# RetNet attention and a leaky-ReLU feed-forward block: second-layer trunk products kept in PSUM over a chunk, and a fourth product by two levels

## The chip, the cores and the metric

The kernel runs on one core of one Trainium2 chip, in fp32. The metric is the device time of one execution in microseconds; a kernel's time is the median of several runs.

## The reference

A recurrent RetNet block feeds two dense layers. What matters here is the second half:

```
state = gamma * state + k_t v_t^T          # per batch and head, 768 positions
y_t   = scale * q_t state
x = y as (3072 tokens, 512)                # 4 batches, 768 positions, 8 heads of 64
h = x @ w_in                               # 512 -> 2048
g = max(0.01 h, h)
out = g @ w_out                            # 2048 -> 512
```

## The kernel before, in words

**Chunks and units.** The 768 positions are cut into six chunks `c` of 128, each with 4 x 128 = 512 tokens; the hidden width 2048 is cut into four units `u` of 512. For each chunk and unit the first layer gives a 512 x 512 hidden block, and the second layer adds its product with the unit's rows of `w_out` to the chunk's output `o` (four blocks of 128 x 512).

**One level and two levels.** Each 512 x 512 product is done with seven products of half-size blocks instead of eight (Winograd's form of Strassen's method). A product done *at one level* is four fp32 matmuls of 128x128 by 256 columns. A product done *by two levels* is cut into seven again: seven fp32 matmuls of 128x128 by 128 columns. A profile shows each fp32 matmul as two MATMUL records and two LDWEIGHTS records.

**The main loop.** Chunks 0 and 1 are done in a first part. From about 249 us on, the loop over `n` (0 to 15; `c, u = 2 + n // 4, n % 4`) does the rest. Step `n` issues, in each engine's program order:

1. `differences(g)`: four VectorE subtractions on the hidden block of unit `n`.
2. `inner(n+1, 0)`: the first layer of the *next* unit, group 0, four products by two levels (28 fp32 matmuls) in PSUM banks 0 to 3; ScalarE copies and VectorE adds take them out. `outer(n+1, 0)` combines them on VectorE.
3. With `u < 2` and another chunk to come ("visiting"), `joint_visit`: the attention output of a pair of batches for the next chunk.
4. `sums_of_x` or `differences` for the next chunk's first-layer operands, on VectorE.
5. The second layer of unit `n`. In steps 0 to 3 and 15 this is `output`: seven products at one level. In steps 4 to 14 (`by_leaves`) four products (M1, M5, M6, M7: the *trunk*) are at one level, and three (M2, M3, M4: the *leaves*) by two levels. `leaf_sums` makes the leaves' operands on GpSimd, four subtractions of 128x384.
6. `scores_of_pair`: attention scores and state sums of the next pair, where there is one.
7. `inner(n+1, 1)`: the first layer, group 1, three products by two levels (21 matmuls), again in banks 0 to 3; then `outer(n+1, 1)`, five VectorE adds and four ScalarE activations.
8. The last trunk product and the leaves (`leaf_steps`), then their addition to `o`.

The order is written out by hand: each engine works through its own queue in the order in which the program issues. In `inner_steps` and `leaf_steps` the order of products is `INNER`: M1, M5, M4, M6, M2, M3, M7; four banks are used, and after M1 ScalarE copies M1's sum from the first bank into the fourth, where M6 and M7 add to it:

```
INNER = (("M1", 0, 0, 0), ("M5", 1, 3, 2), ("M4", 2, 2, 4), ("M6", 3, 4, 3), ("M2", 0, 1, 1),
         ("M3", 1, 5, 5), ("M7", 3, 6, 6))
```

(name, bank among the four, block of the weights, block of the moving operand). VectorE takes M3 once and M7 twice; ScalarE takes the others.

**Trunk and leaves before.** `trunk` puts M1, M5 and M6 + M7 into three banks A, C, B (5, 7, 4), copies A into B after M1, and every unit is added to `o` by VectorE (`o[:, 1]`, `o[:, 2:4]`, and in `trunk_taken` `o[:, 0]` and `o[:, 1:4:2]`). The leaves use banks 6, 7, 2 and 5. Their results lie in SBUF; a DMA issued by GpSimd adds them to `o` (L1283, `accum_op`), except at the chunk's last unit, where VectorE adds them and the output is stored.

**Leaf weights.** Each leaf product needs seven weight blocks per row, three of the original and four sums. In steps 0 to 3 `sums_of_rows` makes the sums on VectorE, four instructions of 128x384 for a unit, and `keep` writes them to DRAM (`leaf_kept`); `load_rows` loads three rows of 448 KB in each step with leaves. The first-layer weights of each step are loaded on the same SP queue (`wa`, `wb` from `kept`).

Of the kernel before, what the change touches and what calls it, by code (L numbers as in the profile page):

```python
# [22 lines left out]
def kernel(  # L23
# [334 lines left out]
    def scores_of_pair(c, b, banks=None, mid=None):  # L358
# [28 lines left out]
        for j in range(2):  # L387
            am = work.tile([128, 2, HP // 2, 2, C // 2], FP32, tag=f"am{j}", name=f"am{j}_{c}_{b}")
            nc.vector.tensor_tensor(
                out=am.rearrange("p b m i t -> p (b m i) t"),  # L390
                in0=at[j].rearrange("p b m i t -> p (b m i) t"),
                in1=mask[:, 0].unsqueeze(1).to_broadcast([128, 2 * HP, C // 2]), op=ALU.mult)
            weights.append(am)
# [7 lines left out]
        if not last:  # L401
            state_of[p] = halves_of_states.pop(0)
            plus(state_of[p], mid, sums[1])
        mid_of[p] = old, mid
# [9 lines left out]
    def joint_visit(c, b, banks=None):  # L414

        later = following(c, b) if c > JOINED else None
        banks = banks or [[bank[k] for k in at] for at in ((1, 2), (0, 7))]
# [193 lines left out]
    def plus(out, a, b):  # L611
        nc.vector.tensor_tensor(out=out, in0=a, in1=b, op=ALU.add)  # L612

    def minus(out, a, b):
        nc.vector.tensor_tensor(out=out, in0=a, in1=b, op=ALU.subtract)  # L615
# [13 lines left out]
    def differences(x, t, last=True):  # L629

        minus(t[:, 0], x[:, 1], x[:, 0])
        minus(t[:, 1], x[:, 3], t[:, 0])
        minus(t[:, 2], x[:, 2], t[:, 1])
        if last:
            last_difference(x)

    def last_difference(x):
        minus(x[:, 1], x[:, 3], x[:, 1])
# [169 lines left out]
    last_three = {}  # L808
# [9 lines left out]
    def new_g(c, u):  # L818
        i = slot[0]
        slot[0] = 1 - i  # L820
        both = work.tile([128, 7, 2, N], FP32, tag=f"g{i}", name=f"g_{c}_{u}")
        last_three[c, u] = both[:, 2:5]
        return u, both[:, 0:4], Reversed(both)
# [309 lines left out]
    def sums_of_x(c, group):  # L1133
# [3 lines left out]
        for blocks, made in (((x[:, 0:1], made[:, :, 0:1]), (t, made[:, :, 1:4])) if group == 0 else  # L1137
# [5 lines left out]
            minus(b12, b22, b12)  # L1143
# [40 lines left out]
    leaf_kept = [dram.tile([128, 3, 7, C], FP32, name=f"leaf_kept_{u}") for u in range(NU)]  # L1184
# [3 lines left out]

    def leaf_rooms():

        free = [flat_of(unit(k)[:, 2:5]) for k in (1, 3, 5)]
        spare = [x2_place[0][:, 21 * C :], streamed_flat[0][:, 21 * C :]]
        more = [spare[i // 2][:, ds(i % 2 * 3 * C, 3 * C)] for i in range(4)]
        return free, spare, [x.rearrange("p (q n) -> p q n", q=3) for x in more]

    def rows_of(u):

        if u < NU - 1:
            return [((0, 3, 1), unit(2 * u + 1)[:, 2:5])]
        return [((0, 3, 2), units[2 * u + 1][1]), ((1, 2, 1), last_s4)]  # L1200

    def sums_of_rows(u):

        free, _, more = leaf_rooms()
        if u == NU - 1:
            more = more[0:2] + [x[:, 7 * C : 10 * C].rearrange("p (q n) -> p q n", q=3)
                                for x in free[0:2]]
        bases = []
        for at, blocks in rows_of(u):
            which = slice(*at)  # L1210
            a11, a21, a12, a22 = (blocks[:, :, k, ts(m, C)] for k in range(2) for m in range(2))
            r = [x[:, which] for x in more]
            plus(r[0], a21, a22)
            minus(r[1], r[0], a11)
            minus(r[2], a12, r[1])
            minus(r[3], a11, a21)
            bases.append((which, blocks))

        def keep():
            for which, blocks in bases:  # L1220
# [4 lines left out]
            for j, r in enumerate(more):  # L1225
                nc.sync.dma_start(out=leaf_kept[u][:, :, 3 + j], in_=r)
        return keep

    def load_rows(n):

        free, spare, _ = leaf_rooms()
        leaf_weights[:] = [x[:, 0 : 7 * C].rearrange("p (j n) -> p j n", j=7)
                           for x in (free[0], free[1], spare[1])]
        for to, kept_rows in zip(leaf_weights, (leaf_kept[at_of(n)[1]][:, i] for i in range(3))):
            nc.sync.dma_start(out=to, in_=kept_rows)

    leaf_weights = []

    def by_leaves(n):
        return n >= NU and n < N2 - 1  # L1240

    def leaf_sums(n):

        free, spare, _ = leaf_rooms()
        made = [x.rearrange("p (q n) -> p q n", q=3)
                for x in (free[0][:, 7 * C : 10 * C], free[1][:, 7 * C : 10 * C],
                          spare[0][:, 0 : 3 * C])]
        three = last_three[at_of(n)]
        b11, b12, b21, b22 = (three[:, :, k, ts(h, C)] for k in range(2) for h in range(2))
        for out, a, b in ((made[0], b12, b11), (made[1], b22, made[0]), (made[2], b21, made[1]),  # L1250
                          (b12, b22, b12)):
            nc.gpsimd.tensor_tensor(out=out, in0=a, in1=b, op=ALU.subtract)
        return [b11, b21, *made, b22, b12]

    def leaf_steps(n, moving):

        ps = [bank[i][:, 0 : 3 * C].rearrange("p (i n) -> p i n", i=3) for i in (6, 7, 2, 5)]
        results = leaf_results()
        for m, q, j, s in INNER:
            for i in range(3):  # L1260
                nc.tensor.matmul(ps[q][:, i], lhsT=leaf_weights[i][:, j], rhs=moving[s][:, i],  # L1261
# [6 lines left out]
            elif m == "M7":  # L1268
                plus(results[:, :, 3], results[:, :, 3], ps[3])
                plus(results[:, :, 2], results[:, :, 2], ps[3])  # L1270
# [5 lines left out]
    def leaf_results():  # L1276
        return flat_of(unit(5)[:, 2:5]).rearrange("p (i q n) -> p i q n", i=3, q=4)

    def leaf_results_taken(c, o, final):

        results = leaf_results()
        if not final:
            nc.gpsimd.dma_start(out=o[:, 0:3].rearrange("p i k n -> p (i k n)"),  # L1283
                                in_=results.rearrange("p i q n -> p (i q n)"), accum_op=ALU.add)
            return
        for i in range(3):
            plus(o[:, i], o[:, i], results[:, i].rearrange("p (k h) n -> p k (h n)", k=2))
            nc.sync.dma_start(out=out[c, i], in_=o[:, i])

    def trunk(c, o, part, first, final):  # L1290

        u, g, gd = part
        ps = {x: room[x] for x in "ABC"}
        for m, x, sa, rhs, start in (("M1", "A", 0, g[:, 0], True), ("M5", "C", 4, gd[:, 0], True),
                                     ("M6", "B", 5, gd[:, 1], False),
                                     ("M7", "B", 1, g[:, 1], False)):
            for i in range(2):
                for k in range(2):
                    nc.tensor.matmul(ps[x][:, i, :], lhsT=block(2 * u + 1, sa)[:, k, ts(i, 128)],  # L1299
                                     rhs=rhs[:, k, :], start=(start and i == 0 and k == 0),  # L1300
                                     stop=(k == 1), skip_group_check=True)
            if m == "M1":
                nc.scalar.copy(out=ps["B"], in_=ps["A"])  # L1303
            elif m == "M6":
                if first:
                    nc.scalar.copy(out=o[:, 1], in_=ps["B"])
                else:
                    plus(o[:, 1], o[:, 1], ps["B"])
            elif m == "M7":
                yield  # L1310
                if first:
# [299 lines left out]
```

## Time and profile before

| | |
|---|---|
| median of 3 runs | 633.93 us (633.60 to 633.94) |
| profiled execution | 633.81 us, span 632.1 us |
| TensorE busy | 624.7 us, 99% |
| VectorE busy | 498.1 us, 79% |
| ScalarE busy | 283.5 us, 45% |
| GpSimd busy | 81.4 us, 13% |
| granted TensorE clock | 1.00 |
| a step with neither visit nor scores | 22.54 us (n = 6, 7, 10, 11, 13, 14) |
| steps 4, 5, 8, 9 | 27.0, 27.0, 27.0, 25.7 us |

PE is TensorE's matmuls and PEld its weight loads, DVE is VectorE, ACT ScalarE, POOL GpSimd, SP the queue that issues most DMAs. `Lnnn` is a line of the kernel, and where a helper such as `plus` (L612) or `minus` (L615) records the instruction, all its users share that line. In a chain, each row is a start, a duration and what ran. In a timeline, each row is a start, a duration, engine, line, operation, output and inputs, shape, count, and in brackets how long the engine had been idle and for whom it waited. A step's length is TensorE's time from one start of inner group 0 to the next.

### The profile page before, as it was taken

How to read it: one execution, taken by the hardware profiler on the slowest of the kernel's cores; microseconds unless marked ns; L12 is line 12 of the kernel's file. 1: busy time of each engine (PE TensorE's matmuls, PEld its weight loads, DVE VectorE, ACT ScalarE, POOL GpSimd, SP SyncE). 2: the span in 40 equal slices, each digit the busy share in tenths (PEclk: the TensorE clock that was granted, in tenths of full speed). 3: DMA queues.
4: the chain of work that ended last, by engine and by line, in shares of the span. 5: the costliest groups of instructions: out<-in, count | busy, mean ns of one | idle time of the engine just before them, and what ended most of it. 6: DMA issues, size and time to landing. Idle time of an engine off the chain costs nothing.

```text
span 632.1 us, 15063 instructions
## 1 busy us (share of the span) xinstructions
PE 624.7 (99%) x6284; PEld 570.5 (90%) x6284; DVE 498.1 (79%) x803; ACT 283.5 (45%) x559; POOL 81.4 (13%) x98
## 2 busy tenths in 40 slices
PE   8999999999999999999999999999999999999997
PEld 5888888888888889899999999999998999999996
DVE  5679769889979976668887768799848889866765
ACT  5876646347443114352442452634434424544540
POOL 2000000000011010101000033313033023033200
PEclk9999999999999999999999999999999999999999
DMA  8941325547772998295964888998479579689724
GB/s 330 404 138 34 133 67 208 163 145 226 260 276 81 334 350 289 89 347 168 340 209 157 280 293 250 342 293 260 157 240 306 159 230 278 206 263 271 192 45 116
DMA packets 103219, 141.18 MB, mean 223 GB/s; under 512 B 4328, under 2 KB 82024, under 8 KB 103152
## 3 DMA queue, kind: packets, MB, share of 16 engines
q1 hardware_dynamic: 101552, 132.53, 63.3%
q0 software_dynamic: 1296, 7.08, 5.6%
q8 instruction: 49, 0.80, 0.5%
q10 hardware_dynamic: 304, 0.62, 0.3%
q14 instruction: 18, 0.15, 0.1%
HBM read 108.49 MB, written 24.64 MB: 211 GB/s over the span
## 4 chain that ended last, share of the span: by engine, by line
PE 90%; DMA 5%; ACT 2%; DVE 2%; issue 0%; SPq 0%; DVEq 0%; ACTq 0%
PE bank L1348 26%; PE bank L1299 12%; PE bank L668 11%; PE bank L1261 8%; PE C_h L668 4%; PE B_o L668 4%; PE A_h L668 4%; PE A_o L668 4%; PE C_o L668 4%; PE B_h L668 4%; PE D_o L668 2%; PE D_h L668 2%; DMA x_words<-in_weights_dram 1%; DMA wa<-kept 1%; DMA in<-in_kv_dram 1%; PE bank L371 1%
## 5 line engine op out<-in xcount | busy, mean ns | idle before, releaser
L612 DVE TENSOR_TENSOR made<-made,bank 128x512 f32<-128x512 f32 (+1 forms) x96 | 56.1, 617 | 39.9 <-PE bank L1348 35.9
L1348 PEld LDWEIGHTS bank<-x,wb 128*128 128x128 f32 x672 | 77.6, 192 | 1.1 <-ACT bank L1352 0.3
L1348 PE MATMUL bank<-x,wb 128*128 128x128 f32 x672 | 77.9, 275 | 0.1
L612 DVE TENSOR_TENSOR o<-o,bank 128x512 f32<-128x512 f32 (+3 forms) x75 | 55.2, 767 | 24.3 <-ACT bank L782 6.2
L615 DVE TENSOR_TENSOR g<-g 128x512 f32<-128x512 f32 x96 | 64.1, 688 | 5.3 <-ACT g L1390 0.6
L1348 PE MATMUL bank<-x,wa 128*128 128x128 f32 x512 | 67.6, 275 | 0.0
L1299 PE MATMUL bank<-g,w 128*128 128x256 f32 x288 | 66.1, 382 | 0.7 <-DVE x L468 0.7
L1348 PEld LDWEIGHTS bank<-x,wa 128*128 128x128 f32 x512 | 62.8, 192 | 0.3
L1299 PEld LDWEIGHTS bank<-g,w 128*128 128x128 f32 x288 | 53.2, 190 | 8.0 <-DVE x L468 1.1
L1348 PE MATMUL bank<-t,wa 128*128 128x128 f32 x384 | 53.4, 275 | 0.1
L1348 PEld LDWEIGHTS bank<-t,wa 128*128 128x128 f32 x384 | 48.0, 192 | 0.3 <-DMA wa<-kept 0.3
L612 DVE TENSOR_TENSOR g<-made 128x512 f32<-128x512 f32 x64 | 44.0, 709 | 3.0
L1352 ACT COPY bank<-bank 128x512 f32<-128x512 f32 (+1 forms) x32 | 16.6, 520 | 60.1 <-PE bank L1348 59.8
L1390 ACT ACTIVATE g<-g 128x512 f32<-128x512 f32 x64 | 38.5, 631 | 8.2 <-DVE g L612 8.2
L668 PE MATMUL bank<-g,w 128*128 128x256 f32 x168 | 38.0, 382 | 0.0
L668 PEld LDWEIGHTS bank<-g,w 128*128 128x128 f32 x168 | 31.3, 190 | 4.2
L668 PE MATMUL bank<-g,last 128*128 128x256 f32 (+1 forms) x148 | 32.6, 375 | 0.0
L668 PEld LDWEIGHTS bank<-g,last 128*128 128x128 f32 x148 | 27.0, 190 | 3.9 <-DVE g L615 0.4
L1261 PE MATMUL bank<-g,w 128*128 128x128 f32 x176 | 26.8, 275 | 0.0
L668 PE MATMUL A_h<-x,w 128*128 128x256 f32 x112 | 26.6, 380 | 0.0
L1303 ACT COPY bank<-bank 128x512 f32<-128x512 f32 x11 | 6.3, 570 | 41.1 <-PE bank L1299 41.1
L1283 POOL DMA_DIRECT2D o<-w x9 | 8.1, 903 | 125.2 <-DVE g L615 65.6
(255 smaller groups left out, 1234.8 us busy)
## 6 DMA issues: line engine op xcount, KB each, us to landing
wa<-kept SPq DMA_DIRECT2D x16, 1344.0 KB, 9.4
raw<-in_weights_dram SPq DMA_DIRECT2D x31, 512.0 KB, 4.4
wb<-kept SPq DMA_DIRECT2D x16, 896.0 KB, 5.5
w<-leaf_kept SPq DMA_DIRECT2D x22, 448.0 KB, 4.6
wa<-kept SPq DMA_DIRECT2D x16, 448.0 KB, 6.1
wb<-kept SPq DMA_DIRECT2D x16, 448.0 KB, 6.3
o<-w POOLq DMA_DIRECT2D x9, 768.0 KB, 9.2
out_dram<-o SPq DMA_DIRECT2D x23, 256.0 KB, 2.5
```

The source lines that it names most:

```text
L371: nc.tensor.matmul(at[j][ts(h, 64), n, m, i], lhsT=x[ts(j, 64), 1, a, ts(h, 64)], rhs=x[ts(j, 64), 0, a, ts(h, 64)], start=(n == 0 and a = ...
L612: nc.vector.tensor_tensor(out=out, in0=a, in1=b, op=ALU.add)
L615: nc.vector.tensor_tensor(out=out, in0=a, in1=b, op=ALU.subtract)
L668: nc.tensor.matmul(to, lhsT=block(w, sa)[:, k, ts(i, 128)], rhs=rhs[:, k, a:z], start=(first and (i == 0 or split) and n == 0 and k == 0), ...
L1261: nc.tensor.matmul(ps[q][:, i], lhsT=leaf_weights[i][:, j], rhs=moving[s][:, i], start=(i == 0 and m in ("M1", "M5", "M4")), stop=True, sk ...
L1283: nc.gpsimd.dma_start(out=o[:, 0:3].rearrange("p i k n -> p (i k n)"), in_=results.rearrange("p i q n -> p (i q n)"), accum_op=ALU.add)
L1299: nc.tensor.matmul(ps[x][:, i, :], lhsT=block(2 * u + 1, sa)[:, k, ts(i, 128)], rhs=rhs[:, k, :], start=(start and i == 0 and k == 0), sto ...
L1303: nc.scalar.copy(out=ps["B"], in_=ps["A"])
L1348: nc.tensor.matmul(ps[q][:, i], lhsT=w[:, j, i], rhs=part_of(moving[i], s), start=(i == 0 and m in ("M1", "M5", "M4")), stop=True, skip_gr ...
L1352: nc.scalar.copy(out=ps[3], in_=ps[0])
L1390: nc.scalar.activation(g[:, i], g[:, i], AF.Prelu, alpha=0.01)
```

## The change

From step 2 to step 14, M1, M5 and M6 stay at one level, but their sums stay in banks A, C and B over all units of a chunk that are done this way: only the first unit's matmul starts the sum. `trunk_taken` takes them out once, at the chunk's last such unit: one ScalarE copy and five VectorE additions. M7 becomes a fourth leaf. The leaves have four blocks in every place where they had three, use banks 6, 2, 0 and 3, and start at step 2 instead of step 4. For units 2 and 3 of chunk 2 (`ON_CHIP`) the weight sums are used from SBUF; GpSimd makes them, in steps 1 and 3. The results of a chunk's first unit are written straight to `o`; those of later units are added to `o` by one VectorE addition of 128x2048 (`add_results`) in the following step. The chunk's stores move to the first step of the next chunk (`finish_chunk`). `outer(n+1, 0)` comes after `joint_visit` or `sums_of_x`; `sums_of_x(c+1, 1)` comes after inner group 0; with `u` = 2 or 3 GpSimd's `leaf_sums` waits for the last of VectorE's `sums_of_x`. The second half of the masks comes last in `scores_of_pair`. The core of the diff (`plus`, `minus`, `differences` and `sums_of_x` also return their last instruction now):

```diff
+    ON_CHIP = range(2, NU)
+    def by_leaves(n):
+        return ON_CHIP[0] <= n < N2 - 1
-        return n >= NU and n < N2 - 1
 def rows_of(u):
-            return [((0, 3, 1), unit(2 * u + 1)[:, 2:5])]
+            return [(slice(0, 4), unit(2 * u + 1)[:, 1:5])]
+        first, second = units[2 * u + 1][0:2]
+        return [(slice(0, 1), first[:, 1:2]), (slice(1, 4, 2), second), (slice(2, 3), last_s4)]
+    def sums_of_rows(u, engine=nc.vector):
+        if u in ON_CHIP:
+            flat = free[1].rearrange("p (r q n) -> p r q n", r=4, q=4)
+            parts = [(slice(0, 4), slice(0, 4), flat)]
+        else:
+            rows = [(slice(0, 1), blocks[:, 0:1]), (slice(1, 4), blocks[:, 1:4])]
...
+        for n in range(4):
+            for which, blocks in rows:
...
+                engine.tensor_tensor(out=r[n], in0=a, in1=b, op=ALU.subtract if n else ALU.add)
 def load_rows(n):
+        for i in range(4):
+            to = free[(1, 3)[i // 2]][:, ds(i % 2 * 7 * C, 7 * C)]
...
+            nc.sync.dma_start(out=to, in_=leaf_kept[at_of(n)[1]][:, i])
+    def leaf_sums(n, behind=None):
+        made = [of_four(leaf_rooms()[x]) for x in ("x2", "wb", "u2")]
+        four = last_four[at_of(n)]
...
+            op = nc.gpsimd.tensor_tensor(out=out, in0=a, in1=b, op=ALU.subtract)
+            if behind is not None:
[...]
+                behind = None
+    TARGETS = (3, 0, 1, 2)
 def leaf_steps(n, moving):
-        ps = [bank[i][:, 0 : 3 * C].rearrange("p (i n) -> p i n", i=3) for i in (6, 7, 2, 5)]
+        ps = [bank[i].rearrange("p (i n) -> p i n", i=4) for i in (6, 2, 0, 3)]
...
+        plus(results[:, :, 2], results[:, :, 2], ps[3])
+        plus(results[:, 2], results[:, 2], results[:, 3])
+        if at_of(n)[1] > 0:
+            unadded.append(lambda: plus(flat_of(os[at_of(n)[0]]), flat_of(os[at_of(n)[0]]),
+                                        results.rearrange("p i q n -> p (i q n)")))
+    def finish_chunk(c):
+        add_results()
+        for i in range(4):
+            nc.sync.dma_start(out=out[c, i], in_=os[c][:, i])
+    def trunk(n, part):
+        first = n == ON_CHIP[0] or u == 0
+        for x, sa, rhs in (("A", 0, g[:, 0]), ("C", 4, gd[:, 0]), ("B", 5, gd[:, 1])):
...
+                                     rhs=rhs[:, k, :], start=(first and i == 0 and k == 0),
+    def trunk_taken(n, o):
+        a, ab, abc = (flat_of_k(leaf_results(n)[:, i]) for i in range(3))
+        nc.scalar.copy(out=a, in_=room["A"])
+        plus(o[:, 0], o[:, 0], room["A"])
+        plus(ab, a, room["B"])
+        plus(abc, ab, room["C"])
+        plus(o[:, 2], o[:, 2], ab)
+        plus(o[:, 1:4:2], o[:, 1:4:2], abc.unsqueeze(1).to_broadcast([128, 2, 2, N]))
 # the loop over n
+        last_leaves = leaves and (u == NU - 1 or n + 2 == N2)
+        if u > 0:
+            add_results()
         if more:
             differences(*gs[n][1:])
...
+        elif leaves and u == NU - 1:
+            behind = sums_of_x(c + 1, 1)
+        if more:
             outer(n + 1, 0)
+        if leaves and u == 0:
+            finish_chunk(c - 1)
+            os[c] = new_o(c)
+        if visiting and u == 1:
+            behind = differences(*xs[c + 1])
+        elif c + 1 < NC and u == 2:
+            behind = sums_of_x(c + 1, 0)
+        if leaves:
+            moving = leaf_sums(n, behind if not scores_next else None)
+            trunk(n, part)
...
+        if last_leaves:
+            trunk_taken(n, os[c])
+        if scores_next and leaves:
+            scores_of_pair(*scores_next, [bank[i] for i in (1, 6, 2, 3)], second_mask_last=True)
...
+        if n in (0, 1):
+            keep.append(sums_of_rows(n))
+        if n in (1, 3):
+            keep.append(sums_of_rows({1: 2, 3: 3}[n], nc.gpsimd))
         if more:
             inner(n + 1, 1)
...
+        if leaves:
+            leaf = leaf_steps(n, moving)
+            last_one = n + 2 == N2
+            for count, ready in ((1, 1), (1, 1), (2, 2)) if last_one else ((4, 3), (1, 1)):
+                products(leaf, count)
+                for _ in range(ready):
+                    later.pop(0)()
+            if last_one:
+                differences(*gs[n + 1][1:])
+            products(leaf, 8)
+            if last_one:
+                add_results()
```

## The prediction

> **What bounds the kernel now.** First the busy shares, then the chain that ended last, then one stretch in order of time on each engine. The shares:
>
> ```profile
> PE 624.7 (99%) x6284; PEld 570.5 (90%) x6284; DVE 498.1 (79%) x803; ACT 283.5 (45%) x559; POOL 81.4 (13%) x98
> ```
>
> TensorE hardly idles, so an edit gains only if it takes work from TensorE. The chain, over step n = 7 of the main loop (start us, us, what):
>
> ```profile
> 427.79 6.25 PE bank L1348 x56
> 434.04 5.18 PE bank L1299 x24
> 439.22 4.69 PE bank L1348 x42
> 443.91 1.73 PE bank L1299 x8
> 445.64 4.69 PE bank L1261 x42
> 450.33 6.25 PE bank L1348 x56
> ```
>
> Weight loads are counted with matmuls: x56 is 28 of each. A step is inner group 0 (6.25), three trunk products (5.18), inner group 1 (4.69), the fourth trunk product M7 (1.73), three leaf products (4.69): 22.54 us, without a gap. From these lines a one-level product costs 5.18/3 = 1.73 us, a two-level one 7 x 0.2233 = 1.56 us. VectorE, GpSimd and one uncontended reference in the same stretch (start, duration, idle before):
>
> ```profile
> 236.26 0.55 DVE L615 TENSOR_TENSOR x<-x 128x384 f32<-128x384 f32 x1
> ...
> 428.76 2.88 DVE L615 TENSOR_TENSOR g<-g 128x512 f32<-128x512 f32 x4
> 431.56 1.36 DVE L615 TENSOR_TENSOR x<-x 128x384 f32<-128x384 f32 x1
> 432.95 2.50 DVE L615 TENSOR_TENSOR x<-x,x 128x384 f32<-128x384 f32 x2
> 435.38 1.35 DVE L615 TENSOR_TENSOR x<-x 128x384 f32<-128x384 f32 x1
> ...
> 443.35 1.62 DVE L612 TENSOR_TENSOR made<-made,bank 128x384 f32<-128x384 f32 x3 [0.91 <-PE bank L1348]
> ```
>
> ```profile
> 431.19 1.31 POOL L1252 TENSOR_TENSOR w<-g 128x384 f32<-128x384 f32 x1 [0.87 <-DVE g L615]
> 432.58 1.19 POOL L1252 TENSOR_TENSOR w<-g,w 128x384 f32<-128x384 f32 x1
> ...
> 465.54 1.00 POOL L1252 TENSOR_TENSOR w<-g,w 128x384 f32<-128x384 f32 x1
> ```
>
> Two things are to be seen. In a step with u = 3, VectorE reaches the eviction of inner group 1 with 0.91 us to spare, and that is all its slack. And `sums_of_x` beside GpSimd's `leaf_sums` takes 1.36 us an instruction instead of 0.55, GpSimd 1.2 to 1.3 instead of 1.00.
>
> [...] the two `mask` products out of PSUM at 465.14 beside GpSimd take 1.29 together. [...] the trace has 688 ns at 512 and 1214 at 1024[...].
>
> **The change part by part.** Time t counts from TensorE's start of the step.
>
> *TensorE.* Steps 4 to 14 turn one product from one level to two: 11 x 0.165 = 1.8 us less. Steps 2 and 3 turn four: 23.03 us (6.25 + 6.91 + 4.69 + 5.18 of that chain) becomes 22.37, 2 x 0.66 = 1.3 less. Together **-3.1 us**. An undisturbed step is 6.25 + 5.18 + 4.69 + 6.25 = 22.37: trunk from 6.25, inner group 1 from 11.43, leaves from 16.12.
>
> *Removed at no gain.* Nine accumulating DMAs (8.1 us of POOL issue, 7.08 MB) and the per-unit trunk evictions lay beside TensorE; the waits on them show on VectorE (6.1 us), not on the chain.
>
> *VectorE with u = 3 (steps 3, 7, 11).* New or wider: `add_results`, the leaf adds at 512 columns, `results[2] += results[3]`, `trunk_taken` with five adds. In queue order, at uncontended paces: two leaf adds and the results add to t = 2.1; `add_results` 2.29, to 4.4; `differences` 2.88, to 7.2; inner evictions 1.87, to 9.05; `sums_of_x` 2.2 (236.26 to 238.47), to 11.2; `outer` 1.42, to 12.6; `trunk_taken` 3 x 0.6 + 0.7 + 1.2, to 16.3; eviction of inner group 1, 1.6, to 17.9; ScalarE's bank copy 0.57, to 18.6. This last matters because the leaf products now use banks 6, 2, 0, 3: leaf M1's copy goes into bank 3, which inner M7 holds until those evictions, and leaf M6, fourth in TensorE's order, is due at 16.12 + 2.68 = 18.8. Queued behind it stand M2, M3, M7 and the next step. So it fits, by 0.2 us, if nothing collides.
>
> It does collide. `leaf_sums` is held behind `sums_of_x` (t = 11.2) and issues four adds of 1.27. They meet four VectorE adds with two SBUF inputs: `outer`'s second waits 1.3, `o[2] += ab` 0.6, `o[1:4:2] += abc` 1.3. Evictions end at 20.95, the copy at 21.6, M6 starts at 21.7: 2.9 us late. A step with u = 2 hands on up to 0.6 more, as its `leaf_sums` start at 14.3 and hold back `outer`'s last five adds. I take **3.2 each for steps 7 and 11, +6.4**; bounds 0 (no collision) and 3.6.
>
> *GpSimd at step 3.* Behind its `leaf_sums` (ending at 16.5 alone, 18.2 with the lock) stand the twelve adds of `sums_of_rows(3)`, whose results the leaves of this very step use: three adds of 0.46, 0.73, 0.46 and gaps for each result. Alone the last result is there at 16.5 + 7.6 = 24.1, where M7 wants it at 21.5: 2.6 us. Alternating with VectorE's `trunk_taken` and five `outer` adds it comes at about 29.7: 8.3 us. This swallows the eviction wait of that step. I take the middle, **+5.5**; the bounds are those two, and 0 if small GpSimd adds cost nothing fixed and no lock were met.
>
> *Steps 6 and 10:* M4 needs `leaf_sums`' third result at 17.9 and gets it at 18.3: **+0.8** for both; bounds 0 and 1.4. *Step 15:* the differences of the last unit, then leaf evictions and `add_results`, stand before the bank 3 copy on VectorE; copy at 27.0, M6 wanted at 25.9: **+1.2**; bounds 0 and 2.
>
> *Costed at nothing.* `joint_visit` ahead of `outer` and other banks for visits and scores: VectorE had 4.3 us idle before the masks at 465.14, and the first mask, the two state adds and the copy end within the 2.0 us until inner M6; without that cover up to 0.8 a visit. `sums_of_rows(0)` and `(1)`: eight adds instead of four, 3.6 us instead of 2.2, within 2.13 and 1.20 us of idle; `sums_of_rows(2)` on GpSimd contends with the second, about 2 us, which `output`'s products hide. On SP: `keep` issues 9, 9, 6 and 10 DMAs instead of 6, 6, 6 and 8, at about 0.8 us each, ahead of loads needed half a step later; four leaf weight loads of 448 KB instead of three, into rooms that nobody reads before t = 16; at step 3 `keep` waits for GpSimd, and the next visit's loads with it. The chunk's stores now wait for `add_results` at step u = 0 and stand before the next `wa` load: issued at about t = 16 instead of 10.5, wanted at 26.4, 9.4 us to land.
>
> *Sum:* -3.1 + 6.4 + 5.5 + 0.8 + 1.2 = +10.8. Against the profiled execution, 633.81 (span 632.1 and 1.7 around it), that is 644.6; the median 633.93 stands 0.12 above it, so I say **644.6**.
>
> **The rivals.** *A, faster:* the lock costs little, since additions land between GpSimd's, or GpSimd's 512-column adds take the 1.02 us of the 128x512 decay products. The decision point is VectorE finishing `trunk_taken` by t = 16.3 at u = 3, which the queue meets exactly without waits; and row sums ready at step 3. Then TensorE's saving stays: 633.8 - 3.1 = 630.7. For it: TensorE's arithmetic is certain. Against: every overlap in this trace shows the alternation. *B, slower, mildly:* the evictions wait, but GpSimd's small adds are cheap: step 3 costs 3 and the others 2 each: -3.1 + 7 + 1 = +5, 638.8. *C, slowest:* on top of the forecast the `wa` load is late behind stores and leaf rows at steps 4 and 8, up to 2 us each, and GpSimd's worst case holds: 633.8 + 10.8 + 2.8 + 4 = 651.4. For it: DMA share was 0.84 to 0.98 in steps 4 to 6; against: 10 us between issue and need.
>
> **How the numbers follow.** Forecast 0.42, B 0.17, C 0.06, A 0.30, and 0.05 that stalls and saving balance. A measurement tells about 0.2% (1.3 us) from no change: faster 0.30, same 0.05, slower 0.65. The forecast's own range is 638 to 649; the whole, 630.4 to 649, leaves out C and the lower edge of A.
>
> **What would show it.** Per step on TensorE: 22.37 at u = 1 and 2 without visits, about 25.6 at steps 7 and 11, near 28 at step 3. In VectorE's line, adds with two SBUF inputs at 1.3 to 1.9 us after `sums_of_x`, and ScalarE's leaf M1 copy released by VectorE. In GpSimd's line twelve adds at step 3 ending after t = 24. Wrong if TensorE runs steps 7 and 11 in under 23 us, or if step 3 stalls on something else than row sums.

## The result and the profile after

The changed kernel takes **643.9 us** (median of 4 runs, 643.61 to 644.20) against 633.79 for the kernel before on the same chip (4 runs, 633.60 to 633.94): ratio 1.016, 95% interval 1.0142 to 1.0177. It is slower by 10.1 us. The profiled execution of the changed kernel took 643.83 us, with a span of 642.0, so 9.9 us more span than before.

The busy shares after, and the chain that ended last by engine, first before and then after:

```profile
PE 626.2 (98%) x6398; PEld 574.8 (90%) x6398; DVE 516.1 (80%) x792; ACT 281.6 (44%) x546; POOL 113.0 (18%) x113
...
PE 90%; DMA 5%; ACT 2%; DVE 2%; issue 0%; SPq 0%; DVEq 0%; ACTq 0%
...
PE 72%; DVE 12%; DMA 7%; POOL 3%; ACT 3%; issue 2%; SPq 1%; DVEq 0%; POOLq 0%; ACTq 0%
```

TensorE is still 98% busy by the first line. The chain tells more: before, TensorE held 90% of it and VectorE 2%; now they hold 72% and 12%, and GpSimd, absent before, holds 3%. Where the time goes is seen in TensorE's waits over the whole span (engine, line, releaser: us in total, times, longest; idle times of 0.15 us and less are not listed):

```profile
PE bank L1309 <- ACT bank L1313: 3.8, 2, 1.9
PE bank L1309 <- POOL w L1248: 3.2, 6, 2.0
...
PE bank L1383 <- DMA wa<-kept: 0.8, 2, 0.5
PE bank L1383 <- issue: 0.5, 1, 0.5
PE bank L1309 <- POOL more_room L1288: 0.4, 1, 0.4
```

L1309 is the leaf matmul, L1313 ScalarE's copy into bank 3, L1248 the row sums, L1288 `leaf_sums`. None of these waits was in the kernel before.

By steps, from one start of inner group 0 to the next on TensorE (us):

| n | before | after | | n | before | after |
|---|---|---|---|---|---|---|
| 0 | 28.24 | 28.39 | | 7 | 22.54 | **26.19** |
| 1 | 27.49 | 27.70 | | 8 | 27.00 | 26.91 |
| 2 | 23.03 | 22.37 | | 9 | 25.72 | 25.39 |
| 3 | 23.03 | **27.58** | | 10 | 22.54 | 23.00 |
| 4 | 26.98 | 27.93 | | 11 | 22.55 | **24.55** |
| 5 | 27.06 | 27.21 | | 12 | 22.87 | 22.38 |
| 6 | 22.54 | 22.65 | | 13 | 22.54 | 22.38 |

Step 14 takes 22.38 instead of 22.54; from there to the end of the span both kernels take 16.2 us.

**Step 7** is the one whose chain the prediction showed. In the changed kernel it starts at 432.63. The chain over it (start us, us, what; "issue" is time without a visible wait):

```profile
442.86 1.03 DVE x L622 x2
443.88 0.61 DVE made L619
...
444.59 1.57 DVE g L619
446.17 0.60 DVE o L619
...
449.13 2.28 DVE o L619
451.41 1.40 DVE made L619 x3
...
452.89 0.58 ACT bank L1313
...
453.52 5.46 PE bank L1309 x32
```

Before, this chain was six rows of TensorE. Now it runs down VectorE's queue, over the trunk's additions to `o` and the eviction of inner group 1 (`made`, x3), through ScalarE's copy to leaf M6. The same stretch in the timelines of VectorE, GpSimd and TensorE:

```profile
434.95 2.29 DVE L619 TENSOR_TENSOR o<-o,w 128x2048 f32<-128x2048 f32 x1
...
442.27 1.15 DVE L622 TENSOR_TENSOR x<-x,x 128x384 f32<-128x384 f32 x2
...
444.59 1.57 DVE L619 TENSOR_TENSOR g<-made 128x512 f32<-128x512 f32 x1
...
448.00 3.41 DVE L619 TENSOR_TENSOR o<-o,w 128x512 f32<-128x512 f32 x2
451.34 1.47 DVE L619 TENSOR_TENSOR made<-made,bank 128x384 f32<-128x384 f32 x3
```

```profile
444.05 1.56 POOL L1288 TENSOR_TENSOR x<-g 128x512 f32<-128x512 f32 x1 [14.37 <-DVE x L622]
445.69 1.61 POOL L1288 TENSOR_TENSOR wb<-g,x 128x512 f32<-128x512 f32 x1
447.38 1.27 POOL L1288 TENSOR_TENSOR more_room<-g,wb 128x512 f32<-128x512 f32 x1
448.62 1.71 POOL L1288 TENSOR_TENSOR g<-g 128x512 f32<-128x512 f32 x1
```

```profile
450.54 1.06 PE L1309 MATMUL bank<-more_room,w 128*128 128x128 f32 x8
453.52 1.19 PE L1309 MATMUL bank<-wb,w 128*128 128x128 f32 x8 [1.92 <-ACT bank L1313]
454.51 4.47 PE L1309 MATMUL bank<-g,w 128*128 128x128 f32 x24
```

`sums_of_x` now runs alone (two in 1.15 us). GpSimd's four adds then take turns with VectorE's second `outer` add (1.57 us) and the two adds `o<-o,w` (3.41 together). M6 is due at 451.60 and starts at 453.52. The last row is one that nothing of this explains: 24 records that take 2.84 us in step 11 take 4.47 here. In busy time by stretch (start:end, length, busy us of PE, PEld, DVE, ACT, POOL with counts, then the granted clock and the DMA share), the 3.41 us stretch of step 7 that holds the wait and the one behind it, then the two stretches of step 11 that share its wait:

```profile
451.11:454.52 3.41, 1.49 (x14) 1.30 (x13) 3.31 (x7) 1.56 (x3) 0.00 (x0) 1.00 1.11 351
454.52:457.93 3.41, 3.41 (x19) 3.41 (x18) 1.58 (x3) 3.13 (x6) 0.00 (x0) 0.50 0.07 16
550.10:553.51 3.41, 2.99 (x27) 2.80 (x26) 3.41 (x4) 0.00 (x0) 1.72 (x2) 1.00 0.50 135
553.51:556.92 3.41, 1.92 (x17) 1.92 (x18) 3.27 (x6) 2.23 (x5) 0.00 (x0) 1.00 0.91 269
```

After the wait in step 7 TensorE ran for 3.41 us at half its clock, which is 1.7 us of work lost. Step 11 has the same wait, 1.91 us, and keeps its clock. That accounts for the difference between 26.19 and 24.55.

**Step 3** starts at 327.26. GpSimd's line and TensorE's leaf M5:

```profile
338.68 1.56 POOL L1288 TENSOR_TENSOR x<-g 128x512 f32<-128x512 f32 x1 [16.03 <-DVE x L622]
...
343.23 1.72 POOL L1288 TENSOR_TENSOR g<-g 128x512 f32<-128x512 f32 x1
344.91 2.12 POOL L1248 TENSOR_TENSOR w<-last 128x128 f32<-128x128 f32 x2
...
353.78 0.46 POOL L1248 TENSOR_TENSOR w<-last_s 128x128 f32<-128x128 f32 x1
```

```profile
346.40 0.49 PE L1309 MATMUL bank<-x,w 128*128 128x128 f32 x2 [1.96 <-POOL w L1248]
```

The row sums stand behind `leaf_sums` and end at t = 27.0, while GpSimd had idled for 16 us before `leaf_sums`.

### The profile page after: what moved, and what is told of

Its sections match the earlier page's. It is cut to its first block, busy times and chain, and to the rows that moved or that the text cites. A ratio compares the mean times of both kernels' runs of the same rounds, so it can differ in the third digit from the quotient of the medians.

```text
span 642.0 us, 15275 instructions
## 1 busy us (share of the span) xinstructions
PE 626.2 (98%) x6398; PEld 574.8 (90%) x6398; DVE 516.1 (80%) x792; ACT 281.6 (44%) x546; POOL 113.0 (18%) x113
## 4 chain that ended last, share of the span: by engine, by line
PE 72%; DVE 12%; DMA 7%; POOL 3%; ACT 3%; issue 2%; SPq 1%; DVEq 0%; POOLq 0%; ACTq 0%
PE bank L1383 18%; PE bank L1309 9%; PE bank L674 6%; PE bank L1349 6%; PE C_h L674 4%; PE B_o L674 4%; PE A_h L674 4%; PE A_o L674 4%; PE C_o L674 4%; PE B_h L674 4%; DVE o L619 3%; DMA wa<-kept 3%; DVE made L619 2%; DVE w L619 2%; DVE g L622 2%
## 5 line engine op out<-in xcount | busy, mean ns | idle before, releaser
L1349 PE MATMUL bank<-g,w 128*128 128x256 f32 x240 | 53.9, 381 | 0.0
L619 DVE TENSOR_TENSOR g<-made 128x512 f32<-128x512 f32 x64 | 50.0, 802 | 3.8 <-DVE made L619 0.5
L1309 PE MATMUL bank<-g,w 128*128 128x128 f32 x400 | 51.4, 282 | 0.7 <-POOL w L1248 0.7
L1349 PEld LDWEIGHTS bank<-g,w 128*128 128x128 f32 x240 | 44.9, 190 | 5.8
L1309 PEld LDWEIGHTS bank<-g,w 128*128 128x128 f32 x400 | 48.6, 198 | 1.4 <-POOL w L1248 1.3
L1288 POOL TENSOR_TENSOR x<-g 128x512 f32<-128x512 f32 x13 | 17.4, 1335 | 158.3 <-DVE x L622 50.9
L619 DVE TENSOR_TENSOR o<-o,w 128x2048 f32<-128x2048 f32 (+2 forms) x18 | 36.0, 2018 | 0.2
L619 DVE TENSOR_TENSOR w<-w,bank 128x512 f32<-128x512 f32 x38 | 25.0, 684 | 9.9 <-PE bank L1309 7.5
L619 DVE TENSOR_TENSOR o<-o,bank 128x512 f32<-128x512 f32 (+2 forms) x38 | 22.6, 626 | 9.4 <-ACT g L1425 3.2
L163 POOL TENSOR_TENSOR in<-in,dec 128x512 f32<-128x512 f32 x2 | 2.2, 1134 | 140.7 <-DMA raw<-in_weights_dram 140.7
L1319 ACT COPY w<-bank 128x512 f32<-128x512 f32 x40 | 23.0, 584 | 7.7 <-PE bank L1309 7.0
```

The source lines that it names most:

```text
L163: engine.tensor_tensor(out=v, in0=v, in1=gk[c].unsqueeze(2).to_broadcast([128, H, D]), op=ALU.mult)
L619: return nc.vector.tensor_tensor(out=out, in0=a, in1=b, op=ALU.add)
L1288: op = nc.gpsimd.tensor_tensor(out=out, in0=a, in1=b, op=ALU.subtract)
L1309: nc.tensor.matmul(ps[q][:, to], lhsT=leaf_weights[i][j], rhs=moving[s][:, i], start=(i == 0 and m in ("M1", "M5", "M4")), stop=True, skip ...
L1319: nc.scalar.copy(out=results[:, :, {"M5": 3, "M4": 2, "M6": 1, "M2": 0}[m]], in_=ps[q])
L1349: nc.tensor.matmul(room[x][:, i, :], lhsT=block(2 * u + 1, sa)[:, k, ts(i, 128)], rhs=rhs[:, k, :], start=(first and i == 0 and k == 0), s ...
```

## The experiments

Theory: at steps 7 and 11 GpSimd's `leaf_sums` and VectorE's adds with two SBUF inputs take turns (in step 7 one took 1.57 us and two took 3.41, where the two adds `w<-w,bank` at 446.69, with one input from PSUM, took 1.40 beside the same GpSimd work), and what they delay is bank 3; step 3 is bound by the row sums behind `leaf_sums`. Rivals: VectorE's queue with u = 3 is simply too long, with or without GpSimd; or holding `leaf_sums` back is itself the mistake. The lock of the prediction and the expectations is this taking of turns. Labels name the kernels; each is an edit of the changed kernel. The kernel before took 633.46 to 633.85 us (medians) beside these runs. Where no number of runs is given, a time is that of one run. Runs of one kernel lie up to 2.9 us apart (633.21 to 636.07 in experiment 9), so the step lengths carry the argument, not the single totals.

**1. GpSimd's sums made tiny in steps 7 and 11** (`e1_small_sums`; one column of 128 is computed, the rest left out):

```diff
+            if n in (7, 11):
+                out, a, b = out[:, :, 0:1], a[:, :, 0:1], b[:, :, 0:1]
             op = nc.gpsimd.tensor_tensor(out=out, in0=a, in1=b, op=ALU.subtract)
```

> Left out: in steps 7 and 11 GpSimd's four subtractions of leaf_sums cover 1 column of 128, so the leaf operands of those steps are mostly stale. GpSimd then reads SBUF for well under 0.3 us an instruction, and all else is as in the changed kernel. Lock theory (VectorE would be in time; it is late because its adds with two SBUF inputs alternate with leaf_sums): VectorE ends the eviction of inner group 1 at about t = 17.9 instead of 20.3, leaf M6 waits 0 to 0.2 us instead of 1.92, steps 7 and 11 take 22.4 to 22.7 us (26.2 and 24.6 in the changed kernel), total about 638. Rival, VectorE simply has too much to do with u = 3 (add_results, five adds of trunk_taken): M6 still waits 1.2 us or more and the steps stay above 23.6.

Measured: 638.72 us (one run); steps 7 and 11 take 22.38. VectorE's line in step 7 (this kernel's step starts at 433.58):

```profile
445.53 0.69 DVE L619 TENSOR_TENSOR g<-made 128x512 f32<-128x512 f32 x1
...
448.06 1.82 DVE L619 TENSOR_TENSOR o<-o,w 128x512 f32<-128x512 f32 x2
449.80 1.47 DVE L619 TENSOR_TENSOR made<-made,bank 128x384 f32<-128x384 f32 x3
```

GpSimd's four sums take 0.50, 0.72, 0.21 and 0.21 us there, the first two longer than expected. On VectorE, same instructions, same order: 0.69 instead of 1.57, 1.82 instead of 3.41, and the eviction begins at t = 16.2 instead of 18.7. VectorE's queue alone fits: the copy into bank 3 ends at t = 18.4, 0.5 us before M6 starts. The collisions are the cause. The rival of a queue that is too long falls.

**2. The two colliding adds put behind the eviction** (`e2_split_taken`):

```diff
 def trunk_taken(n, o):
...
         plus(abc, ab, room["C"])
+    def trunk_added(n, o):
+        ab, abc = (flat_of_k(leaf_results(n)[:, i]) for i in (1, 2))
         plus(o[:, 2], o[:, 2], ab)
         plus(o[:, 1:4:2], o[:, 1:4:2], abc.unsqueeze(1).to_broadcast([128, 2, 2, N]))
...
             inner(n + 1, 1)
+            if last_leaves:
+                trunk_added(n, os[c])
```

> trunk_taken is cut in two: the two additions that read SBUF twice (o[2] += ab, o[1:4:2] += abc) are issued after inner group 1 and its evictions instead of ahead of them; nothing is left out. If the wait of leaf M6 is the path (bank 3 held by inner M7 until VectorE reaches it), the evictions move ahead by the two adds[...], 3.3 us: M6 waits 0 to 0.3, steps 7 and 11 take 22.4 to 22.7, step 3 stays at about 27.5 since GpSimd's row sums bound it, total 643.9 - 3.6 - 2.0 = about 638.3 (637 to 639.5). Rival, the delay only moves: outer's five adds and the leaf evictions then come 2 to 3 us later, the next step's bank 3 copy or differences wait, and the total stays above 641.

Measured: 639.33 us (4 runs, 639.21 to 640.15), ratio to before 1.0093 (1.0077 to 1.011). Steps 7 and 11 take 22.37. In step 7:

```profile
444.70 1.57 DVE L619 TENSOR_TENSOR g<-made 128x512 f32<-128x512 f32 x1
...
448.47 1.62 DVE L619 TENSOR_TENSOR made<-made,bank 128x384 f32<-128x384 f32 x3 [0.28 <-PE bank L1386]
450.01 1.82 DVE L619 TENSOR_TENSOR o<-o,w 128x512 f32<-128x512 f32 x2
```

The collision with `outer` is still there (1.57), but now VectorE waits 0.28 us for TensorE at the eviction: its slack is back. And the two adds, moved past the last of GpSimd's, take 1.82. So it was these adds' place, not the presence of a collision. The kernel loses 1.6 us at its end, where TensorE waits 0.18 and 0.42 us for ScalarE's copies of leaf results and 0.68 for a copy of ScalarE in step 15; the adds also move in step 14, which experiment 5 undoes.

**3. Tiny row sums for unit 3** (`e3_small_rows`; one column is computed, the rest left out):

```diff
+                if u == 3:
+                    r[n], a, b = r[n][:, :, 0:1], a[:, :, 0:1], b[:, :, 0:1]
                 engine.tensor_tensor(out=r[n], in0=a, in1=b, op=ALU.subtract if n else ALU.add)
```

> Left out: GpSimd's twelve additions of sums_of_rows(3) at step 3 cover 1 column of 128, so unit 3's summed weights are mostly stale. If the row sums bound step 3, its waits for GpSimd go and the eviction wait shows that they hid: step 3 takes 24.2 to 24.8 us (26.2 if the granted clock drops after the wait as in step 7) instead of 27.6, total about 641. Rival, step 3 is bound by VectorE's evictions like steps 7 and 11 and the row sums lie beside them: step 3 stays at 27 or more.

Measured: 643.57 us, no gain in the total, yet step 3 falls from 27.58 to 24.62. So the row sums bound it. What is left isn't the wait that the expectation named. TensorE's one listed wait in the step is still for a row sum, the first, which stands behind `leaf_sums` (this kernel's lines are two further on):

```profile
348.59 1.16 PE L1311 MATMUL bank<-x,w 128*128 128x128 f32 x8 [1.69 <-POOL w L1250]
...
350.68 1.13 PE L1311 MATMUL bank<-wb,w 128*128 128x128 f32 x8
```

```profile
349.97 0.57 ACT L1315 COPY bank<-bank 128x512 f32<-128x512 f32 x1 [4.79 <-DVE made L619]
```

ScalarE's copy into bank 3 ends at 350.54, at the same t = 20.8 as in step 7 of the changed kernel, and M6 (the second row) starts 0.14 us later. Without the wait for the row sum M6 would have been due some 1.7 us earlier and would have waited for this copy instead: two waits lie on top of one another. Experiment 8 shows the second one alone. The total does not show the gain for two reasons of the clock: in this execution the part ahead of the loop took 2.3 us longer (251.11 to 248.80 at step 0), with a stretch at half clock from 8.0 to 11.4 us that the changed kernel's profile doesn't have; and the later half clock fell in step 11 (26.17), not in step 7 (24.55).

**4. `leaf_sums` not held back** (`e4_no_behind`):

```diff
-            moving = leaf_sums(n, behind if not scores_next else None)
+            moving = leaf_sums(n)
```

> leaf_sums no longer waits for the last of sums_of_x or of the chunk differences: GpSimd starts it once the differences of g are there (t = 7.4). Lock theory: the alternation only moves from outer and trunk_taken to sums_of_x, which takes 1.3 us an instruction again instead of 0.5; M6 in steps 7 and 11 waits about as long (1 to 2.5 us), steps 6 and 10 come down to 22.4 as M4 finds its operand, step 3 gains 2 to 4 us because the row sums start at about t = 13; total 639 to 642. Rival, holding leaf_sums back is what costs: all steps with u = 3 fall to 22.4 to 23, total under 637.

Measured: 643.17 us. Steps 6 and 10 fall to 22.38 and 22.73; steps 7 and 11 are 24.92 and 24.93. Step 3, expected 2 to 4 us shorter, takes 28.27, of which 1.7 are lost to half clock (350.66 to 354.08). VectorE's `sums_of_x` in step 7, then TensorE in step 3, which now waits for `sums_of_x` too:

```profile
442.79 1.49 DVE L622 TENSOR_TENSOR x<-x 128x384 f32<-128x384 f32 x1
444.32 3.05 DVE L622 TENSOR_TENSOR x<-x,x 128x384 f32<-128x384 f32 x2
```

```profile
341.10 3.62 PE L1383 MATMUL bank<-x,wb 128*128 128x128 f32 x30 [0.73 <-DVE x L622]
350.43 1.84 PE L1309 MATMUL bank<-wb,w 128*128 128x128 f32 x8 [3.03 <-ACT bank L1313]
```

The collisions moved from the trunk's adds to `sums_of_x`: about 1.5 us an instruction instead of 0.55. Holding `leaf_sums` back pays nothing with u = 2 and isn't what costs with u = 3.

**5. The adds behind the eviction only where u = 3** (`f1_split_u3`; `trunk_added` follows `trunk_taken` at once in step 14):

```diff
+            if last_leaves and u == NU - 1:
+                trunk_added(n, os[c])
```

> Only for u = 3 (steps 3, 7, 11) do the two adds of trunk_taken with two SBUF inputs, o[2] += ab and o[1:4:2] += abc, come behind the evictions of inner group 1; step 14 keeps them where the change put them. Theory (they stand in front of the copy into bank 3, each waiting a turn behind GpSimd): steps 7 and 11 at 22.4 us, step 3 unchanged at 27.6 (bound by row sums), and the end of the kernel as in the changed kernel, so about 643.9 - 3.8 - 2.2 = 637.9 us. Rival (the 1.5 us that e2_split_taken lost at its end were not due to the split in step 14): step 14's start at 597 as there, but 639.3 again.

Measured: 638.09 us; steps 7 and 11 at 22.38 and 22.37, step 3 at 27.58. The end is as in the changed kernel, and the total is as expected to 0.2 us.

**6. Step 3 begun differently** (`f2_row_order`: as 5, `leaf_sums` free at n = 3, leaves in the order M1, M4, M2, M5, M6, M3, M7 there; `f3_early_sums`: as that, and `leaf_sums` free with u = 2 too):

```diff
+        for m, q, j, s in [INNER[k] for k in (0, 2, 4, 1, 3, 5, 6)] if n == 3 else INNER:
```

> f1_split_u3, and in step 3 alone leaf_sums is not held behind sums_of_x, and the three leaf products that need no row sums (M1, M4, M2) run first. Theory (step 3 waits for GpSimd's twelve row sums and nothing else): they begin near t = 13 instead of 17 and the first is wanted at 18 instead of 16.8, so step 3 falls from 27.6 to 22.5-24.5 us and the time to about 634.5. Rival (each GpSimd add just takes another turn with VectorE, wherever it starts): row sums still end after t = 23, step 3 at 26 or more, 636.5 or more.

> f2_row_order, and leaf_sums is not held in steps with u = 2 (6 and 10) either. Theory: M4 finds its sum there, steps 6 and 10 at 22.4-22.7 instead of 22.65 and 23.0, and steps 7 and 11 stay at 22.4, as e4_no_behind lost there only through the adds that the split moves: about 0.5 us less than f2_row_order. Rival: earlier GpSimd adds hold back VectorE's sums_of_x (inner group 0 of the next step waits for it), and steps 7 and 11 grow to 23-25.

Measured: 636.28 and 636.57 us. Step 3 takes 27.12 in both: the theory's 22.5 to 24.5 was wrong, and so was the rival's reason, as the row sums end at t = 21.3. `sums_of_x`, now beside GpSimd, is 0.74 us late, and with it the eviction of inner group 1. M2, moved forward, goes into the first of the four banks (bank 6 here), so it needs ScalarE's copy out of that bank into bank 3, and waits 1.71 us for it; two more waits, 0.39 and 0.91, are for ScalarE's copies of leaf results. Steps 6 and 10 fell to 22.38 and 22.39 in the second, and steps 7 and 11 stayed at 22.38 and 22.37; steps 5 and 9 gave back the gain (27.22 and 25.16 instead of 26.81 and 24.81). Step 4 took 0.8 less, and what lies ahead of step 1 took 0.8 more.

**7. Stores meant to be later, which did not move** (`f4_stores_later`, meant as the changed kernel with the first chunk's four stores behind inner group 1 in step 4):

```diff
     def finish_chunk(c):
-        add_results()
...
         if leaves and u == 0:
-            finish_chunk(c - 1)
+            add_results()
+            if c > 1:
+                finish_chunk(c - 1)
...
                 ahead(c + 2, 2 * u + i)
+            if leaves and u == 0 and c == 1:
+                finish_chunk(c - 1)
```

> The changed kernel with the four stores of the first finished chunk, in step 4, issued behind inner group 1 and its loads instead of ahead of them. Step 4 has 0.5 to 1.0 us of TensorE idle with no releaser near t = 25 in every variant so far. Theory (it is a fetch of instructions that queues behind the DMA traffic of these stores): that idle time goes or moves, step 4 at 27.0-27.4 instead of 27.9-28.4. Rival (it is the order of instructions on TensorE, or a fetch that any traffic delays): the same idle time, step 4 at 27.9-28.4. Both: steps 7 and 11 as in the changed kernel, total within 1 us of 643.9.

The edit moves nothing: in this loop `c` runs from 2 to 5, so `c > 1` always holds and `c == 1` never does. The stores are issued at t = 13.33 to 14.70 of step 4, in the changed kernel at 13.32 to 14.70, and SP, VectorE and GpSimd run the same instructions in the same order as there. So the theory of the stores is untested, and the run is one more execution of the changed kernel.

Measured: 641.74 us; the idle time without a releaser is 0.98 us (0.54 in the first profile), step 4 takes 28.36 (27.93). This idle time (0.5 to 1.2 us near t = 20 of step 4) is in both executions of the changed kernel and in eight of the eleven variants, with 0.23 us in experiment 9, and not in the kernel before. In the changed kernel a 16 KB packet of the instruction queue (372.00 to 372.93) ends 0.9 us ahead of it, but the profile has 50 such packets, 13 us apart on average, most without a stall. That such a packet causes it is not shown; what it is stays open. The total is 2.2 us lower with the same instructions, 1.6 of it in step 7: the half clock fell in step 3, where TensorE waits for GpSimd anyway (27.59), and step 7 kept its clock (24.56).

**8. Row sums ahead of `leaf_sums`** (`g2_rows_first`, one move; `g3_split_rows`, with 5; `g1_all`, with 5 and `leaf_sums` free with u = 2):

```diff
         part = gs.pop(n)
         behind = None
+        if n == 3:
+            keep.append(sums_of_rows(3, nc.gpsimd))
...
-        if n in (1, 3):
-            keep.append(sums_of_rows({1: 2, 3: 3}[n], nc.gpsimd))
+        if n == 1:
+            keep.append(sums_of_rows(2, nc.gpsimd))
```

> The changed kernel with one move: in step 3 the twelve row sums of unit 3 are issued on GpSimd ahead of leaf_sums, at the start of the step, where GpSimd idles for 12 us before leaf_sums. Theory (step 3 is bound by these sums standing behind leaf_sums): the row sums are done by t = 10, and the step falls from 27.6 to what the late eviction of inner group 1 leaves, about 24.5 as in e3_small_rows; total about 641. Rival (they now alternate with VectorE's leaf adds, add_results and differences, and sums_of_x comes late): a wait for x or g appears in front of inner group 1, and the step stays at 26 or more.

> g2_rows_first and f1_split_u3 together: the two adds behind the evictions where u = 3, and the row sums first in step 3. Theory: both stalls go, step 3 at 22.4-23.5 instead of 27.6, steps 7 and 11 at 22.4, so 638.1 - 4.5 = about 633.6, level with the kernel before. What stays above the TensorE saving of 3.1 us would then be steps 4 (0.9 more than before) and 3. Rival (waits displaced, as in f2_row_order): step 3 at 25-27, 636 to 637.

> g3_split_rows with leaf_sums not held where u = 2 (steps 6 and 10). Theory: 0.3 to 0.9 us less than g3_split_rows, about 633.0, slightly faster than the kernel before (ratio 0.998 to 1.000). Rival (steps 4, 5 and 9 give it back, as in f3_early_sums): no less than g3_split_rows.

Measured: 644.31 (one run), 635.41 (6 runs, ratio 1.0032, 1.0020 to 1.0043) and 635.31 us (5 runs, ratio 1.0037, 1.0024 to 1.0051). Step 3 takes 29.12, 24.64 and 24.61. In the first, TensorE's waits are 1.40 us (M4, for `leaf_sums`) and 1.97 (M6, for bank 3), and 6.8 us at half clock follow, 3.4 us of work: 22.37 + 3.37 + 3.4 = 29.1. M6's row:

```profile
350.25 2.07 PE L1309 MATMUL bank<-wb,w 128*128 128x128 f32 x8 [1.97 <-ACT bank L1313]
```

This is the eviction wait that the row sums hid in the changed kernel. So the move alone took the waits for row sums away (the step would take 25.7 at full clock) and left this one, with a new one for M4. With the adds behind the eviction the bank 3 wait and the half clock are gone; 1.10 us for M4 and 0.48 for a copy of a leaf result stay. Why M4 waits, GpSimd's line of `g3_split_rows` shows:

```profile
331.71 0.85 POOL L1248 TENSOR_TENSOR w<-last 128x128 f32<-128x128 f32 x1 [8.67 <-DMA leaf_kept<-w]
334.31 0.91 POOL L1248 TENSOR_TENSOR w<-last 128x256 f32<-128x256 f32 x1 [1.75 <-DMA leaf_kept<-w]
```

The room for the new row sums is the old one's: they wait until unit 2's sums have been stored, t = 4.1 and 6.7 of the step. Freeing `leaf_sums` where u = 2 is not shown to pay: 635.31 against 635.41.

**9. Those stores earlier** (`h1_keep_early`, as `g1_all`; they are issued 7 to 9 us earlier):

```diff
             products(begun, 7)
+        if n == 2:
+            keep.pop(0)()
```

> g1_all with the stores of unit 2's row sums issued ten us earlier in step 2, behind inner group 0 instead of behind inner group 1. In g3_split_rows the first row sum of step 3 waited for such a store until t = 3.7 and the next until t = 6.3, so that leaf_sums came behind them and leaf M4 waited 1.1 us. Theory: the row sums start with the step, leaf_sums with sums_of_x's end, M4's wait goes, step 3 at 22.4-23.5 instead of 24.6: about 634.1, within 0.2% of the kernel before. Rival (started earlier, they take their turns from add_results and differences instead): trunk product C or inner group 1 waits for VectorE, step 3 at 24.5 or more, 635.3 or more.

Measured: **634.02 us** (14 runs, 633.21 to 636.07) against 633.85 for the kernel before (19 runs), ratio 1.0004 (0.9993 to 1.0014). Step 3 takes 23.10. GpSimd's line there, and all that TensorE waits for between 300 and 600 us:

```profile
326.92 0.73 POOL L1248 TENSOR_TENSOR w<-last 128x256 f32<-128x256 f32 x1 [1.85 <-DMA leaf_kept<-w]
...
336.02 0.90 POOL L1248 TENSOR_TENSOR w<-last_s 128x128 f32<-128x128 f32 x1
340.67 1.58 POOL L1288 TENSOR_TENSOR x<-g 128x512 f32<-128x512 f32 x1 [3.74 <-ACT bank L1390]
```

```profile
PE bank L1386 <- issue: 0.2, 1, 0.2
```

The row sums end at t = 9 (the step starts at 327.87), and `leaf_sums` no longer follows them but `sums_of_x`, which ends at 340.52 (the view names a copy of ScalarE's that ends 0.1 us later). TensorE has no wait above 0.15 us in step 3, yet the step is 0.73 longer than 22.37. The chain there runs over the moved adds into ScalarE's copies of leaf results:

```profile
348.29 1.56 ACT L1319 COPY w<-bank 128x512 f32<-128x512 f32 x3 [1.53 <-DVE o L619]
```

The inputs of the moved adds lie in the room that these copies fill, so the copies wait for the adds. Four moves, none of which takes work away, return the 10 us together; the arithmetic of the change and its instruction counts are untouched. The kernel is then level with the one before, not faster.

## Why the prediction was right

The forecast was 644.6; the profiled execution took 643.83, the median is 643.9. The direction and its two causes were right; some sizes agree only in the sum. One reading was off without harm to the sum: x56 in the chain is 56 MATMUL records, two for each of 28 matmuls, and counts no weight loads. By the prediction's own steps:

| step of the sum | predicted | measured |
|---|---|---|
| TensorE, 2 to 14 | -3.1 | -3.1: bare steps 22.37 or 22.38, step 2 from 23.03 to 22.37 |
| steps 7 and 11 | +6.4 | +6.0: 26.19 and 24.55 less 22.37 each |
| step 3 | +5.5 | +5.2: 27.58 less 22.37 |
| steps 6 and 10 | +0.8 | +0.9: 22.65 and 23.00 less 22.37 each |
| step 15 | +1.2 | 0: 16.2 us in both kernels |
| the rest, costed at nothing | 0 | +0.9 |
| sum | +10.8 | +9.9 |

*Prices.* These were the author's estimates, and the runs bear them out. `add_results` was put at 2.29 us and takes 2.29 (step 7, 434.95); a line through the 688 ns at 512 columns and 1214 at 1024 of VectorE in the kernel before gives 2.27. GpSimd's 512-column add was put at 1.27, and where nothing collides it takes 1.27 (step 7, 447.38); its 256-column add at 0.73, and it takes 0.73 (experiment 9, 326.92); its 128-column add at 0.46, and alone it takes 0.45 or 0.46 (step 3, 353.78).

*Steps 7 and 11: right mechanism, the wait too long.* The chain of step 7 is the predicted one, link by link: `outer`'s second add, the trunk's adds, the eviction, ScalarE's copy into bank 3, M6. But M6 started at t = 20.9, not 21.7, and was 1.9 us late, not 2.9. The mis-sized term is the three collisions, put at 3.2 us; they cost 0.9 (1.57 less 0.69) and 1.6 (3.41 less 1.82 in experiment 1), 2.5 together. Nor did a step with u = 2 hand anything on: `sums_of_x` of step 7 ends at t = 11.25, as the queue without it has it. That the sum came out all the same is luck: 1.7 us at half clock in step 7, which the prediction did not have. Without them these steps would cost 4.3 and the kernel would take 642.2, still in the stated range.

*Step 3: right mechanism, near its middle value.* The last row sum ended at t = 27.0, between the bounds of 24.1 and 29.7; the middle was a choice between them, not worked out. The sentence that the row sums swallow the eviction wait is shown by experiment 8: with the row sums in front, M6 waits 1.97 us for bank 3 in this step.

*Step 15: wrong.* The copy into bank 3 was put at t = 27.0, counted from the start of step 14, against a need at 25.9. It starts at 628.97 and ends at t = 26.1, TensorE waits 0.14 us for it, and the way to the end is as long as before. The term that was too big is what stood ahead of the copy: it waits for the differences and the leaf evictions (to 628.88), but `add_results` runs only from 629.71, behind it.

*Costed at nothing:* the visiting steps 4, 5, 8 and 9 changed by +0.95, +0.15, -0.09 and -0.33; with TensorE's saving of 0.66 taken off that is +1.3. On average this is inside the 0.8 a visit that was the bound without cover; step 4 alone is above it (+1.1), half a microsecond of it the idle time of experiment 7 that stays open. Step 9 also lost a wait of 0.70 us for VectorE that the kernel before had, so the visits cost more than their sum shows. The `wa` load behind stores and leaf rows (rival C) is late by 0.5 us at most, in step 9. Steps 0 and 1 cost 0.4 more; the loop began 0.4 earlier, and inner group 1 of step 12 had taken 0.3 longer in the kernel before (5.19 us instead of 4.85).

*The rivals.* A (630.7) needed collisions that cost little and row sums in time; experiment 9 provides both and reaches 634.0. So its end was wrong too: of the 3.1 us, step 3 still keeps 0.7, steps 6 and 10 0.4, the four visiting steps take as long together as before (0.6), and steps 0 and 1, the way to the loop and the end take about 0.3 each. These figures are of the profiled execution, the fastest of the 14 (span 631.1, before 632.1); over all runs the median spans are level, 632.0 and 632.1. B (638.8) took GpSimd's small adds to be cheap; a 128-column add is 0.45 us alone, 0.90 in turns, and 1.43 once.

## What to carry to other kernels

Before placing an instruction with two SBUF inputs on VectorE beside GpSimd work, ask what stands behind it in VectorE's queue that frees a bank: putting the eviction first was worth about 6 us here (1.7 of them clock) and cost nothing in steps 7 and 11, though at the kernel's end the same move cost 1.6. By contrast, an earlier start of GpSimd's work moved its collisions to other instructions (experiment 4: two of `sums_of_x` in 3.05 us instead of 1.15). Where GpSimd's results are used in the same step, follow the room they are written to back to the store that empties it; here that store, not GpSimd, set the start. And a saving of 0.5% on the bounding engine has to be weighed against the slack of every queue that the freed memory or the moved sums draw on; a queue with 0.2 us to spare by its own sum has none.

## What the runs showed of the hardware

A wait of about 2 us on TensorE cost up to twice its length. In step 7 of the changed kernel the wait of 1.92 us was followed by 3.41 us at a granted clock of 0.50, and cost 3.6; in step 11 a wait of 1.91 us was followed by a clock of 1.00, and cost 1.9. Over the fourteen profiles of this case full clock gave way to half clock six times in the loop, five times for 3.41 us and once, in `g2_rows_first`, for 6.8:

| kernel | half clock from (us) | TensorE idle in the 3.41 us before it (us) |
|---|---|---|
| changed kernel | 454.52 | 1.92 |
| `e1_small_sums` | 348.90 | 1.76 |
| `e3_small_rows` | 554.10 | 1.91 |
| `e4_no_behind` | 350.66 | 3.03 |
| `f4_stores_later` | 346.30 | 1.97 |
| `g2_rows_first` | 349.44 | 2.25 |

The idle time alone doesn't settle it: step 11 of the changed kernel had as much in one wait and kept its clock, and `e3_small_rows` went to half clock at 8.0 us, ahead of the loop, after 3.50 us in which TensorE idled 1.08. What decides is not shown. By this the time jumped by 1.7 us between edits that have nothing to do with it, as experiment 3 shows, and between executions of the same instructions, as experiment 7 does.

The other surprise is how closely the two engines' adds take turns. In experiment 1 VectorE's add `g<-made` runs from 445.53 to 446.22, and GpSimd's second one-column add, begun at 445.58, ends at 446.30: 0.72 us where the next two take 0.21. The VectorE add takes 0.69 us there and 1.57 beside full GpSimd adds.
